# A quarter of the descriptor space for GpSimd's indirect transfers

## Chip, cores and metric

The kernel runs on one core of a Trainium2 chip. The metric is the device time of one execution in microseconds (us); of several runs the median counts. The engines are named as the profile names them: PE is TensorE (PEld its weight loads), DVE VectorE, ACT ScalarE, POOL GpSimd, SP SyncE; a q behind a name (POOLq, SPq) marks what the engine's sequencer does itself, such as semaphore instructions, DRAINs and the issue of DMAs.

## What is computed

Attention with a local window and a few global keys, and behind it a mixture of experts in which each token goes to one expert. Cut to what matters:

```python
# q, k, v: (4, 8, 768, 64); n_global 8, n_local 96; N = 3072 tokens, D = 512, E = 8 experts, F = 1024
scores = q @ k.T / 8 + alibi_bias            # kept where global, or 0 <= row - col < 96
a = softmax(where(keep, scores, -1e9))
x = (a @ v) as (N, D)
logits = x @ w_gate + modality_bias[modality_id]
e_idx = argmax(logits); gate_w = softmax(logits)[e_idx]
for e in range(E):
    mask = e_idx == e
    out[mask] = gate_w[mask] * (relu(x[mask] @ w1[e]) @ w2[e])
```

## The kernel before

*Attention stage.* 24 steps of 128 query rows each (`step`, four batches of six). A step loads `qt`, `kt`, `va`, `vl` on SyncE's queue, makes scores `s` (line 209), a biased minimum on VectorE (224), the exponential on ScalarE (240), transposes `pr` (254), multiplies by the values (279, 290) and writes 128 rows to `x_rows` in device memory (328). Gate logits and the routing are worked in between: for each token a row of its own in the list `ids_sorted`, sorted by expert, is written by GpSimd (`route_c`, 445), one indirect transfer for 128 tokens, 24 in all.

*Expert stage.* Eleven slots of one expert's tokens each: three of 256 tokens that start before the attention ends (e0 to e2), three of 512 (b0 to b2), two of 256 (c0, c1) and three small ones (g0 to g2, the last of 32 rows), in the order e0, e1, e2, b0, g0, b1, g1, c0, b2, c1, g2. For each slot SyncE loads the sorted token numbers (632) and the weights (660, 662), GpSimd gathers the tokens' rows from `x_rows` 128 at a time (`gather_x`, 640, 25 transfers), TensorE transposes them (`x_t`, 699), ScalarE and VectorE split rows and weights in a high and a low part (`split`, 686 and 687), TensorE multiplies (717 to 719 or 733 to 735, then 776 to 778), and `fin` scales the result on ScalarE (845) and writes its rows to `out` with an indirect transfer of GpSimd (846, 25 transfers). So GpSimd makes 74 indirect transfers: 24, 25 and 25, all but two of them of 128 rows.

*Order.* TensorE's and ScalarE's order is written out by hand (`manual_schedule`), in the attention stage VectorE's and GpSimd's too. SyncE's order, and in the expert stage VectorE's and GpSimd's, is set by a planner when the kernel is built.

*Storage.* The descriptor space of GpSimd's indirect transfers lies at the bottom of each partition, 16,384 bytes by default (line 1592 passes no size). Above it come the constants and small pools, then the attention pools `a1` (57,088 bytes: `kt`, `va`, `vl`, `tbl`, `pr`), `pp` (29,952 bytes: `qt`, `sc`, `pT`, `xr`, `xT`) and `a2` (9,024 bytes). The pools of the expert stage are laid from the other end downwards: `mp`, `wraw`, `wspa`, `xgp` and `idp` down to byte 117,152, and once the attention pools are closed `wspb` (76,192 to 117,152; the third cast of an expert's second weight matrix goes to 92,576 to 96,672), `wrawb` and `mp2` (down to 35,232). Where they lie over closed attention pools, the first user of a tile waits for the last user of the tiles below it (`reuse_waits="tile"`).

*Closing.* Behind the last slot each engine reads a flag and branches over a part that runs only for other inputs (1566, 1567); then come the closing waits, DRAINs and barriers of all engines, which the profile puts down to line 1637.

## Time and profile before

| | us |
|---|---|
| median of 3 runs (lowest, highest) | 444.78 (444.1, 445.35) |
| the profiled execution's own time | 443.69 |
| its span, from the first to the last instruction | 441.8 |
| TensorE busy | 426.5 |
| VectorE busy | 287.7 |
| ScalarE busy | 256.8 |
| GpSimd busy | 104.4 |

All rows are of the profiled execution. Busy time counts arithmetic and GpSimd's transfers, not the sequencers' work. A stretch of the span in which an engine is busy all the time is limited by that engine; one in which no engine is busy is limited by waits, which stand with the sequencers.

### The profile page before, as it was taken

What the parts mean: (1) busy time and instruction counts of PE and PEld (TensorE: products, weight loads), DVE (VectorE), ACT (ScalarE), POOL (GpSimd) and SP (SyncE); (2) the same over time, 40 slices, a digit from 0 to 9 for tenths busy, and PEclk for the clock granted to TensorE, in tenths of its full rate; (3) what the DMA queues carried; (4) which work ended last, traced back from release to release, by engine and by line L of the source; (5) the groups of instructions that cost most, each with busy time, mean ns of one, the idle gap of its engine ahead of it and who ended that gap; (6) DMA issues with size and microseconds to landing.
All of it is one profiled execution on the core that took longest, in us unless ns stands there. A gap on an engine that the chain in (4) does not pass through costs nothing.

```text
span 441.8 us, 12144 instructions
## 1 busy us (share of the span) xinstructions
PE 426.5 (97%) x4584; PEld 363.5 (82%) x4584; DVE 287.7 (65%) x1000; ACT 256.8 (58%) x511; POOL 104.4 (24%) x173
## 2 busy tenths in 40 slices
PE   8899999999999999999999999999999999999990
PEld 7788898898888989898888788887889888879850
DVE  7787887789798589999895347355355735702500
ACT  5888888888885374546446357345374644513420
POOL 6010023122523367241211133000332220011010
PEclk9999999999999999999999999999999999999997
DMA  8999999998878467659129767536667662351510
GB/s 241 314 317 349 359 333 322 319 287 263 275 242 304 168 218 299 208 164 357 55 61 343 286 197 222 199 97 203 216 202 256 219 216 96 118 214 49 192 35 27
DMA packets 53155, 97.63 MB, mean 221 GB/s; under 512 B 8143, under 2 KB 21967, under 8 KB 53088
## 3 DMA queue, kind: packets, MB, share of 16 engines
q1 hardware_dynamic: 48416, 83.92, 57.5%
q0 software_dynamic: 4672, 12.85, 8.0%
q8 instruction: 38, 0.62, 0.6%
q14 instruction: 29, 0.24, 0.2%
HBM read 82.37 MB, written 14.45 MB: 219 GB/s over the span
## 4 chain that ended last, share of the span: by engine, by line
PE 71%; issue 18%; POOL 3%; ACT 2%; DVE 2%; DMA 1%; POOLq 0%; SPq 0%
PE pt L254 7%; PE s L209 7%; PE x L290 6%; PE phb L718 3%; PE phb L719 3%; PE phb L717 3%; PE x L279 3%; PE pob L776 3%; PE tx L335 3%; PE phe L733 3%; PE pob L777 3%; PE pob L778 3%; PE phe L735 3%; PE phe L734 3%; PE poe L776 3%
## 5 line engine op out<-in xcount | busy, mean ns | idle before, releaser
L240 ACT ACTIVATE pr<-sc,nmx 128x168 f32<-128x168 f32 x192 | 67.6, 427 | 9.4 <-DVE nmx L224 6.8
L224 DVE CUSTOM_DVE_ANT_0 sc<-s,tbl 128x168 f32<-128x168 f32 x192 | 53.0, 329 | 16.7 <-PE s L209 15.0
L209 PE MATMUL s<-kt,qt 64*64 64x168 f32 x768 | 39.7, 313 | 0.6 <-DVE nmx L224 0.6
L254 PE MATMUL pt<-ident,pr 128*128 128x128 f32 x288 | 36.9, 277 | 1.1 <-issue 1.1
L719 PE MATMUL phb<-xhb,alb 128*128 128x512 f32 x96 | 37.8, 393 | 0.0
L718 PE MATMUL phb<-xlb,ahb 128*128 128x512 f32 x96 | 37.6, 392 | 0.0
L717 PE MATMUL phb<-xhb,ahb 128*128 128x512 f32 x96 | 37.6, 391 | 0.0
L846 POOL DMA_INDIRECT out<-obb,oib x12 | 12.6, 1047 | 99.5 <-ACT obb L845 97.7
L254 PEld LDWEIGHTS pt<-ident,pr 128*128 128x128 f32 x288 | 31.0, 141 | 5.9 <-issue 5.0
L209 PEld LDWEIGHTS s<-kt,qt 64*64 64x64 f32 x768 | 30.2, 133 | 6.4 <-DVE nmx L224 2.2
L261 ACT COPY pT<-pt 128x512 f32<-128x512 f32 x52 | 29.6, 588 | 8.0 <-PE pt L254 7.2
L445 POOL DMA_INDIRECT ids_sorted<-tki,pi x24 | 24.8, 1033 | 39.4 <-ACT pr L240 28.0
L290 PE MATMUL x<-va,pT 128*64 128x65 f32 x768 | 27.7, 224 | 0.0
L733 PE MATMUL phe<-xhe,ahe 128*128 128x256 f32 x96 | 27.5, 287 | 0.0
L734 PE MATMUL phe<-xle,ahe 128*128 128x256 f32 x96 | 27.2, 283 | 0.0
L735 PE MATMUL phe<-xhe,ale 128*128 128x256 f32 x96 | 27.2, 283 | 0.0
L290 PEld LDWEIGHTS x<-va,pT 128*64 128x64 f32 x768 | 24.4, 137 | 1.6
L721 ACT ACTIVATE hhb<-phb 128x256 fp32r<-128x256 f32 x24 | 9.3, 386 | 26.4 <-PE phb L719 26.4
L722 DVE SCALAR_TENSOR_TENSOR hlb<-phb,hhb 128x256 fp32r<-128x256 f32 x24 | 10.1, 422 | 20.6 <-ACT hhb L721 20.5
L718 PEld LDWEIGHTS phb<-xlb,ahb 128*128 128x128 f32 x96 | 18.0, 188 | 4.5 <-DVE xlb L703 0.4
L719 PEld LDWEIGHTS phb<-xhb,alb 128*128 128x128 f32 x96 | 18.0, 188 | 3.9
L717 PEld LDWEIGHTS phb<-xhb,ahb 128*128 128x128 f32 x96 | 18.0, 188 | 3.9
(408 smaller groups left out, 1146.0 us busy)
## 6 DMA issues: line engine op xcount, KB each, us to landing
va<-in_vr SPq DMA_DIRECT2D x24, 520.0 KB
kt<-in_ks SPq DMA_DIRECT2D x24, 272.0 KB
qt<-in_qs SPq DMA_DIRECT2D x24, 256.0 KB
x_rows<-xr SPq DMA_DIRECT2D x24, 256.0 KB
vl<-in_vo SPq DMA_DIRECT2D x48, 81.2 KB
rawe0a<-in_moe_w SPq DMA_DIRECT2D x4, 512.0 KB
rawe0b<-in_moe_w SPq DMA_DIRECT2D x4, 512.0 KB
rawe1a<-in_moe_w SPq DMA_DIRECT2D x4, 512.0 KB
```

Of the source, the lines that this page charges most:

```text
L209: nc.tensor.matmul(ps[g][64 * half : 64 * half + 64, c0 : c0 + W], qt[hs, hp, 64 * half : 64 * half + 64], kt[hs, hp, w0 : w0 + W], start= ...
L224: V.tensor_tensor_reduce(out=sc, in0=pss[n][g][:, c0 : c0 + W], in1=(tbl0 if n % NB == 0 else tbl)[:, hh, :], op0=ALU.add, op1=ALU.min, sc ...
L240: last[0] = nc.scalar.activation(pr[:, h * (PRW - W) : h * (PRW - W) + W], scs.pop((n, hh)), AF.Exp, bias=blk[n][:, hh : hh + 1], scale=-1.0,)
L254: nc.tensor.transpose(tp[:, j * P : (j + 1) * P], prs[(NP * n + hp) % NPR][:, o : o + P], ident)
L261: last[0] = nc.scalar.copy(pT.rearrange("p a b -> p (a b)"), tp)
L290: nc.tensor.matmul(px[h][64 * half : 64 * half + 64, hp * D1 : (hp + 1) * D1], pT_of(n, hp, 2 * h)[:, 64 * half : 64 * half + 64], va[r][: ...
L717: nc.tensor.matmul(ph, hi[:, fs], s.xh[:, c, :], start=(c == 0), stop=False)
L718: nc.tensor.matmul(ph, hi[:, fs], s.xl[:, c, :], start=False, stop=False)
L719: nc.tensor.matmul(ph, lo[:, fs], s.xh[:, c, :], start=False, stop=(c == 3))
L733: nc.tensor.matmul(o, hi[:, fs], s.xh[:, c, :], start=(c == 0), stop=False)
L734: nc.tensor.matmul(o, hi[:, fs], s.xl[:, c, :], start=False, stop=False)
L735: nc.tensor.matmul(o, lo[:, fs], s.xh[:, c, :], start=False, stop=(c == 3))
```

## The change

The program is built with a descriptor space of 4,096 bytes of each partition for GpSimd's indirect transfers, in place of the default of 16,384. Nothing else is edited. The constants and the attention pools, which are laid from below, come to lie 12,288 bytes lower (of `xr`, for instance, 104,832 to 110,976 becomes 92,544 to 98,688); the pools of the expert stage keep their places.

```diff
-    nc = _bacc.Bacc("TRN2", target_bir_lowering=False, num_devices=1)
+    nc = _bacc.Bacc("TRN2", target_bir_lowering=False, num_devices=1, dynamic_dma_scratch_size=4096)
```

## Rows read from the trace of the kernel before

**Rows 1.** The page: span, then busy us (share of the span) xinstructions

```profile
span 441.8 us, 12144 instructions
PE 426.5 (97%) x4584; PEld 363.5 (82%) x4584; DVE 287.7 (65%) x1000; ACT 256.8 (58%) x511; POOL 104.4 (24%) x173
```

**Rows 2.** Stretches: from:to, length, busy PE, PEld, DVE, ACT, POOL, clock, DMA, GB/s

```profile
136.00:142.00 6.00, 5.64 (x115) 4.67 (x110) 5.44 (x14) 3.75 (x7) 0.46 (x1) 1.00 0.73 240
142.00:240.00 98.00, 98.00 (x606) 86.14 (x607) 83.03 (x255) 50.09 (x76) 34.33 (x29) 1.00 0.59 208
240.00:418.00 178.00, 177.64 (x917) 148.14 (x919) 89.20 (x113) 87.17 (x128) 31.25 (x28) 1.00 0.56 187
431.00:441.80 10.80, 0.00 (x0) 0.00 (x0) 0.00 (x0) 0.69 (x1) 0.99 (x1) 0.73 0.08 28
```

**Rows 3.** GpSimd in order of time: start us, us, what, idle before it

```profile
193.96 0.98 POOL L640 DMA_INDIRECT xgb<-x_rows,uib  x1 [0.56 <-issue]
195.25 1.20 POOL L640 DMA_INDIRECT xgb<-x_rows,uib  x1 [0.30 <-issue]
...
431.98 0.99 POOL L846 DMA_INDIRECT out<-obc,oic  x1 [2.81 <-ACT obc L845]
```

**Rows 4.** Line 1567: operation xcount, ns min/median/max, first and last start us

```profile
L1567 POOLq INC_SWDGE_SEM  x1: 1675/1675/1675, 433.1 to 433.1; - x1
```

**Rows 5.** Line 1637, the closing instructions, columns as in rows 4

```profile
L1637 POOLq EVENT_SEMAPHORE  x4: 17/17/17, 441.0 to 441.7; - x4
L1637 POOLq DRAIN  x3: 46/107/6117, 434.8 to 441.5; - x3
L1637 SPq DRAIN  x3: 7/7/13, 435.7 to 441.2; - x3
...
L1637 PEldq DRAIN  x2: 8/8/8, 431.5 to 441.3; - x2
L1637 ACTq DRAIN  x2: 8/8/8, 434.3 to 441.2; - x2
```

**Rows 6.** SyncE's waits from 430 us on: us in total, times, longest

```profile
SPq L1637 <- PEq L1637: 5.9, 2, 5.4
SPq L1637 <- DMA out<-obc,oic: 0.2, 1, 0.2
```

**Rows 7.** Line 1592, the opening instructions, columns as in rows 4

```profile
L1592 POOLq DRAIN  x1: 194/194/194, 0.4 to 0.4; - x1
```

**Rows 8.** The indirect transfers by line, columns as in rows 4, and their landings

```profile
L445 POOL DMA_INDIRECT ids_sorted<-tki,pi x24: 956/973/1469, 69.6 to 175.4; - x24
...
L640 POOL DMA_INDIRECT xgb<-x_rows,uib x12: 949/1094/2022, 194.0 to 331.5; - x12
L640 POOL DMA_INDIRECT xge<-x_rows,uie x6: 954/1398/1841, 129.3 to 166.5; - x6
...
L640 POOL DMA_INDIRECT xgg<-x_rows,uig x3: 985/985/1504, 230.0 to 353.2; - x3
...
DMA to landing us min/median/max: 3.2/6.9/8.6
...
L846 POOL DMA_INDIRECT out<-obb,oib x12: 985/1006/1293, 249.7 to 403.9; - x12
L846 POOL DMA_INDIRECT out<-obe,oie x6: 985/1094/1433, 176.7 to 218.5; - x6
L846 POOL DMA_INDIRECT out<-obc,oic x4: 983/998/1036, 357.3 to 432.0; - x4
L846 POOL DMA_INDIRECT out<-obg,oig x3: 899/1022/1129, 275.9 to 428.3; - x3
```

**Rows 9.** Transposes of b0's rows, first block's casts, last write of rows, by start

```profile
206.16 0.60 PE L699 MATMUL mtb<-ident,xgb 128*128 128x128 f32 x4
...
154.04 1.99 ACT L686 CAST bhe<-rawe0b 128x1024 fp32r<-128x1024 f32 x2
...
143.29 0.35 SPq L328 DMA_DIRECT2D x_rows<-xr  x1
```

## Prediction

> **What bounds the kernel now.** I read the busy line of the page first: TensorE works for 426.5 of 441.8 us [rows 1]. The table by stretch then says where the other 15.3 us lie. Between 142 and 240 us TensorE lacks nothing, between 240 and 418 us 0.36 us, in the change of stages from 136 to 142 us 0.36 us; but from 431.0 to 441.8 us it does nothing at all [rows 2]. So no cost or saving on another engine moves the time in the body unless it makes TensorE wait, and there is one stretch of 10.8 us, the tail, in which the time is set by something else. That is where to look for a change that touches no matmul.
>
> In the tail the last scale and the last write of rows to `out` are over soon: GpSimd takes the last indirect transfer at 431.98 us for 0.99 us [rows 3], then an instruction of line 1567 for 1.675 us, to 434.8 us [rows 4]. The closing instructions, all put down to line 1637, show who is late: ScalarE's first DRAIN stands at 434.3, TensorE's at 431.5, SyncE's, which comes behind all its waits for transfers, at 435.7. GpSimd's first DRAIN starts at 434.8 and takes 6.117 us, to 440.9, and GpSimd's next semaphore instruction is at 441.0 [rows 5]. SyncE's last wait for a transfer is 0.2 us long, and then it stands 5.4 us for an engine [rows 6], which by these times is GpSimd (the view names another). So the rows have landed by 435.7 us and for the 5.3 us up to 441.0 the whole chip waits for one instruction of GpSimd.
>
> **What is in that instruction.** GpSimd has three more DRAINs, before its first transfer (0.194 us) and behind the long one (0.107 and 0.046 us) [rows 5, 7]. All four run with the same descriptor space, so its size alone isn't what takes 6 us; what differs is that 74 indirect transfers have gone since the DRAIN before: 24 scatters of token numbers, 25 gathers of rows, 25 writes of results [rows 8]. Nor is it the flight of the last one, by SyncE's 435.7. I take it that GpSimd goes through the records of the transfers that it still holds in that space, which costs 6.117/74 = 0.083 us each. In the body nothing says that it had to free records: the 74 take between 0.90 and 2.02 us [rows 8], at the end as at the start.
>
> **The change, part by part.** (1) *Fewer records at the end.* With a quarter of the space, GpSimd must free old records on the way, and holds fewer when it drains. How many isn't in the trace. Upper end of the gain: the DRAIN shrinks until SyncE's 435.7 us is late instead, 5.3 us. Lower end: the small space, too, holds all 74, no gain. If the default was just filled, a quarter of 74, 18.5, stays: 18.5 x 0.083 = 1.53 us, the DRAIN ends at 434.8 + 1.5 = 436.3 instead of 440.9, which is 4.6 us. I take 4.6, near the upper end, because a space that holds more than 74 at once is offset if old records are freed many at a time when it runs full; both ends stay for the range.
>
> The Trainium skill has sizes for this, which no row here shows. "DMA: Bandwidth & Descriptors", section "Terms", gives 16 bytes for a descriptor, and its section "The descriptor swizzle" nine per DMA engine for a transfer of 128 partitions. An estimate from that page: 4,096/16 = 256 places hold 28 such transfers, 16,384 bytes 113. If they were freed one at a time, 28 would be left, 2.3 us, and the gain 3.8 us; if all at once, at the 29th and the 57th, 18 would be left, and it is 4.6.
>
> (2) *The freeing moves into the body.* Some 55 records x 0.083 = 4.6 us of GpSimd's time, spread over transfers from 150 us on. GpSimd is busy for 24% of the span [rows 1]. The work that hides it is the matmuls between a gather and the transposes that read it. The tightest such gather behind the first 18 transfers is the first of block b0: issued at 193.96 us, transposed at 206.16; the longest landing of its kind is 8.6 us, so 206.16 - 193.96 - 8.6 = 3.6 us of cover [rows 3, 8, 9]. Even half of the 4.6 us in one place would stay under it. Cost 0; without that cover 1.0 us at most (4.6 - 3.6).
>
> (3) *A wait for space.* A transfer that finds the space full waits until an older one has landed. Lower bound 0: landings take at most 8.6 us and two starts on GpSimd are at least 1.2 us apart [rows 3, 8], so at most some 7 transfers are under way at once, against the 18 that a quarter holds at the least. Upper bound: it waits for all before it, 8.6 us. I take 0, since 7 is far from 18. Queued behind the waiting instruction on GpSimd are the next gathers, writes and scatters, and TensorE's transposes wait for the gathers alone.
>
> (4) *Storage.* The attention pools lie above the descriptor space and move down by 12,288 bytes; the expert stage's pools, laid from the other end, stay. So the expert tiles `bhe`, `ble`, the raw weights and `xhb` reuse storage of other attention tiles than before. The waits that this takes away can give TensorE at most its 0.36 us from 136 to 142 us [rows 2]. A new one: the third cast of the first block (the second of the pair at 154.04, so 155.1 us) now takes the place of the row tiles `xr`, whose last write starts at 143.29; with the longest landing of any row, 8.6 us, it is over at 151.9, 3.2 us earlier [rows 9]. I take 0, between -0.4 and +0.4. Instructions are neither added nor removed in the source; the planner may order SyncE, VectorE and GpSimd anew in the expert stage, which the same 0.36 us bound as gains and which I leave in the range as a loss of up to 0.5 us.
>
> Sum: -4.6 + 0 + 0 + 0. On the profiled execution's 443.69 us (span 441.8 and 1.9 around it) that is 439.1. The median of the runs is 444.78, 1.1 us higher, so the forecast there is 440.2 us.
>
> **The rivals.** *The DRAIN doesn't shrink:* its 6.1 us are a fixed price once any transfer has gone, or all 74 still fit. For it: there is no row with a DRAIN behind a few transfers. Against it: nothing has been left to wait for since 435.7, and a fixed price of that size shows in none of the other three. Time: 444.8, no change. The Trainium skill speaks for this: "VectorE: DVE Perf Modes", section "The DRAIN you can't avoid", counts the DRAINs at a program's start and end as boilerplate of about 12 ns on every engine, whatever the kernel. By that rule the descriptor space couldn't matter and the time would be 444.8; the trace agrees for ScalarE (8 ns) and SyncE (7 to 13 ns) and differs for GpSimd's 6,117 ns [rows 5].
>
> *Only part goes:* records are freed one by one and 25 to 57 of the 74 stay: 6.117 - 25 x 0.083 = 4.0 us down to 6.117 - 57 x 0.083 = 1.4 us of gain, 440.8 to 443.4, some 442 us. The trace has nothing for or against.
>
> *The small space stalls GpSimd:* a full space makes it wait for everything in it to land, just ahead of b0's first gather, and the DRAIN stays. 8.6 us less the 3.6 us of cover is 5.0 us in which TensorE stands: 449.8 us. It decides from a wait of 3.6 us on. Against it stand the 7 under way at most.
>
> **How the numbers follow.** Forecast (gain 4.0 to 5.3): 0.58. Part goes: 0.20. No change: 0.16. Stall: 0.06. About 0.3%, 1.3 us, is what a measurement of this kernel can tell from none; so faster 0.78, same 0.16, slower 0.06. Low end: the lowest run, 444.1, less 5.3 is 438.8. High end: with 3.8 it would be 441.0; to leave out no more than 2 in 10 it takes in the whole second rival, up to the border of no change, 443.4.
>
> **What the changed profile would show.** Step 1: GpSimd's long DRAIN on the closing line falls from 6.1 to about 1.5 us, and the stretch behind TensorE's last matmul from 10.8 to about 6.2; SyncE's first DRAIN stays some 4.7 us behind that matmul. Step 2: indirect transfers behind the first 18 take a little longer in sum, or a few take some us more. Step 3: TensorE's idle time from 142 to 418 us stays near 0.4 us. Step 4: casts and loads keep their order around 136 to 160 us. A DRAIN of 6 us again would make the forecast wrong in step 1; TensorE idle ahead of `mtb` would in step 3.

## The result and the profile after

The changed kernel takes 438.14 us in the median of 4 runs (437.77 to 440.06), the kernel before 444.44 us in 4 runs beside it (443.81 to 445.35). The ratio is 0.987, with a 95% interval of 0.984 to 0.990: faster, by 6.3 us between the medians. That is the way that was forecast and more of it, and 0.7 us below the low end of the range. The profiled execution took 440.06 us, of which the span is 438.0; that of the kernel before took 443.69 and 441.8.

First the busy line of the page after, against [rows 1]:

```profile
span 438.0 us, 12145 instructions
PE 426.7 (97%) x4584; PEld 363.9 (83%) x4584; DVE 287.3 (66%) x1000; ACT 256.8 (59%) x511; POOL 103.3 (24%) x173
```

No work has gone: TensorE's busy time differs by 0.2 us, GpSimd's by 1.1. The arithmetic, the loads and the transfers are the same on all five engines, and so is their order, but for two matmuls on TensorE that run side by side. So the 3.8 us by which the span is shorter are waits. The table by stretch shows whether they lay in the body (columns as in [rows 2]):

```profile
136.00:142.00 6.00, 4.35 (x78) 3.62 (x74) 4.76 (x12) 3.71 (x7) 0.62 (x1) 1.00 0.53 163
142.00:240.00 98.00, 98.00 (x644) 86.17 (x645) 83.15 (x254) 49.13 (x75) 34.34 (x29) 1.00 0.59 206
240.00:418.00 178.00, 177.57 (x902) 148.65 (x901) 89.33 (x114) 88.15 (x130) 30.18 (x28) 1.00 0.56 190
```

They didn't. From 142 to 418 us TensorE lacks 0.43 us, as before (0.36); in the change of stages it lacks 1.65 in place of 0.36, so the body of this profile is longer. TensorE's waits from 130 to 142 us name the 1.3 us:

```profile
PE lp L344 <- issue: 1.3, 1, 1.3
```

"issue" is time in which the engine waited for nothing that the profile shows. This row is in neither of the next two profiles of a kernel with 4 KB (e1, e2), so I don't put it down to the change.

What has gone lies in the tail. GpSimd's last transfer after, against [rows 3]:

```profile
433.50 0.99 POOL L846 DMA_INDIRECT out<-obc,oic  x1 [2.81 <-ACT obc L845]
```

And the closing instructions, against [rows 4] (line 1567) and [rows 5] (line 1637):

```profile
L1567 POOLq INC_SWDGE_SEM  x1: 395/395/395, 434.6 to 434.6; - x1
...
L1637 POOLq EVENT_SEMAPHORE  x4: 17/17/17, 437.2 to 437.9; - x4
L1637 POOLq DRAIN  x3: 46/107/1946, 435.1 to 437.8; - x3
L1637 SPq DRAIN  x3: 7/7/13, 437.2 to 437.5; - x3
...
L1637 PEldq DRAIN  x2: 8/8/8, 433.0 to 437.5; - x2
L1637 ACTq DRAIN  x2: 8/8/8, 435.9 to 437.5; - x2
```

Read them from the start of the last transfer. GpSimd's instruction of line 1567 falls from 1.675 to 0.395 us, its long DRAIN from 6.117 to 1.946. The DRAIN now ends 435.1 + 1.9 = 437.0, and SyncE, whose DRAIN stands behind its waits for transfers, is there at 437.2: SyncE is the last one now. From the last transfer's start to GpSimd's next semaphore instruction it was 441.0 - 432.0 = 9.0 us and is 437.2 - 433.5 = 3.7, so 5.3 us less. From TensorE's DRAIN to the end of the span it was 441.8 - 431.5 = 10.3 us and is 438.0 - 433.0 = 5.0, again 5.3 less. The profiles' difference, 3.8, is this 5.3 less the 1.5 us by which this body is longer.

SyncE's waits from 430 us on show the same turn, against [rows 6]:

```profile
SPq L1637 <- DMA out<-obc,oic: 1.5, 1, 1.5
SPq L1637 <- PEq L1637: 0.7, 2, 0.5
```

It waits 1.5 us for the landing of the last rows. Its two waits for the other engines come to 0.7 us in place of 5.9: one of 0.5 us stands in both profiles, and the one of 5.4 us is down to 0.2.

### The profile page after: what moved, and what is told of

Its sections match the earlier page's. It is cut to its first block, busy times and chain, and to the rows that moved or that the text cites. A ratio compares the mean times of both kernels' runs of the same rounds, so it can differ in the third digit from the quotient of the medians.

```text
span 438.0 us, 12145 instructions
## 1 busy us (share of the span) xinstructions
PE 426.7 (97%) x4584; PEld 363.9 (83%) x4584; DVE 287.3 (66%) x1000; ACT 256.8 (59%) x511; POOL 103.3 (24%) x173
## 4 chain that ended last, share of the span: by engine, by line
PE 73%; issue 18%; ACT 2%; POOL 2%; DVE 2%; DMA 1%; POOLq 0%; SPq 0%; DVEq 0%
PE s L209 8%; PE pt L254 7%; PE x L290 6%; PE phb L718 3%; PE phb L719 3%; PE phb L717 3%; PE x L279 3%; PE pob L776 3%; PE tx L335 3%; PE phe L733 3%; PE pob L777 3%; PE pob L778 3%; PE phe L735 3%; PE phe L734 3%; PE poe L776 3%
## 5 line engine op out<-in xcount | busy, mean ns | idle before, releaser
L279 PE MATMUL x<-vl,pT 40*64 40x65 f32 x768 | 20.5, 222 | 1.5 <-ACT pT L261 0.8
```

The source lines that it names most:

```text
L279: nc.tensor.matmul(px[h][64 * half : 64 * half + 64, hp * D1 : (hp + 1) * D1], pT_of(n, hp, 1)[hs, 64 * half : 64 * half + 64], vl[r][hs, ...
```

## The experiments

The theory: GpSimd keeps a record of each indirect transfer until it frees it, pays at the end by the number of records that it still holds, and a small space makes it free them on the way. The rivals: it pays by the size of the space, not by the count; the other storage gives a part; the body is faster too. For the first, two profiles decide nothing: a DRAIN of 0.56 us and 0.35 for each KB goes through both.

**e1, the changed kernel again.**

> The changed kernel once more, 4 KB of descriptor space. Theory: the end alone is shorter, by 5.3 us (from the last indirect transfer's start to GpSimd's next semaphore instruction 9.0 us before, 3.7 us after); the rest of the 6.3 us between the first medians is spread from run to run. Then the difference of the medians comes down towards 5.3 us with more runs, a time of about 438.7 against 444.2, and the 1.3 us that TensorE stood at 136 us in the first profile is not there, or is elsewhere. Rival: the body is faster too, by 1 us; then the difference stays at 6.3 us.

Measured: 443.82 us (6 runs) against 449.33 (11 runs) of the kernel before on that chip, so 5.5 us; ratio 0.9866 (0.9839 to 0.9893). The line-1567 instruction took 0.396 us, the DRAIN 1.962; from TensorE's last matmul to the end 5.59 us, where the kernel before has 10.83. All profiles of one kernel have the same end within some 0.2 us (10.83 twice before; 5.57, 5.59 and 5.79 after); what moves between them is the body.

**e2, 4 KB with every tile in its old place.**

```diff
-    warm = const.tile([P, P], BF16, name="warm")
+    warm = const.tile([P, P + 6144], BF16, name="warm")[:, 0:P]
```

> 4 KB of descriptor space, and 12,288 unused bytes above it, so that every tile lies where it lies in the kernel before. Theory: the storage does nothing; the same time as the changed kernel in the same call within 0.7 us, and the same closing DRAIN of about 1.9 us and line-1567 instruction of 0.4 us. Rival, the moved pools give about 1 us of the gain: the time is 1 us above the changed kernel's, with the same end.

Measured: 443.41 us, ratio 0.9865 (0.9827 to 0.9903) beside e1's 0.9866; 0.396 and 1.987 us at the end. The 12,288 bytes by which the pools move have no part in the gain that these runs can tell.

**e3 and e4, 8 KB and 2 KB.**

```diff
-    nc = _bacc.Bacc("TRN2", target_bir_lowering=False, num_devices=1, dynamic_dma_scratch_size=4096)
+    nc = _bacc.Bacc("TRN2", target_bir_lowering=False, num_devices=1, dynamic_dma_scratch_size=8192)
```

> 8 KB of descriptor space. Theory, GpSimd pays by the record still held: with 8 KB it frees once, at about the 57th transfer, and some 25 are left: a DRAIN of 2.1 us at 0.083 each (2.9 if there is a fixed part of 1.3 us), a line-1567 instruction of 0.6 us, and one indirect transfer that starts about 1 us late. Rival, it pays by the size of the space: the two profiles at 16 and 4 KB give 0.56 us and 0.35 us for each KB, so 3.3 us for the DRAIN, and 0.8 us for the other. Time by the first 438 to 439, by the second 440.

> 2 KB of descriptor space. Theory, by the record: about 11 left, as with 4 KB, so the DRAIN stays at 1.9 us and the line-1567 instruction at 0.4; more freeing on the way, each time shorter (some 0.2 us before a transfer); the time is that of the changed kernel, since SyncE's waits set the end. Rival, by the size: a DRAIN of 1.25 us and 0.2 us. Second rival, a space that small makes a transfer wait for earlier ones to land: single indirect transfers start microseconds late and TensorE stands, over 440.

Line 1567 and the closing DRAINs of e3, then of e4 (columns as in [rows 4]):

```profile
L1567 POOLq INC_SWDGE_SEM  x1: 696/696/696, 438.6 to 438.6; - x1
...
L1637 POOLq DRAIN  x3: 46/107/2477, 439.3 to 442.4; - x3
L1637 SPq DRAIN  x3: 7/7/13, 441.3 to 442.1; - x3
```

```profile
L1567 POOLq INC_SWDGE_SEM  x1: 416/416/416, 438.6 to 438.6; - x1
...
L1637 POOLq DRAIN  x3: 46/107/2017, 439.0 to 441.7; - x3
L1637 SPq DRAIN  x3: 7/7/13, 441.1 to 441.4; - x3
```

With 2 KB the two instructions are those of 4 KB (e1), and even 0.02 and 0.06 us longer, where a price by size wanted 1.25 us: that rival falls. With 8 KB the DRAIN is 2.48, not 3.3, but 0.4 more than 25 x 0.083; and the transfer that was to start 1 us late isn't there. Ratios 0.9870 (0.9837 to 0.9903) and 0.9857 (0.9828 to 0.9886): the times can't tell the three sizes apart, the ends can (from the last matmul 6.21 us with 8 KB, 5.63 with 2 KB).

**e5, 16 KB and a DRAIN in the middle.** This one keeps the space and takes the records away.

```diff
                     tc.declare_no_dep(ins.ins, prev.ins, reason="each token has a row of its own")
                 fins.append(ins)
+            if s.name == "c0" and t == 1:
+                behind(nc.gpsimd.drain(), ins)
```

> 16 KB of descriptor space as before, and one DRAIN of GpSimd added in the expert stage, right behind the 67th indirect transfer, ahead of some 30 us in which GpSimd has nothing to do. Theory, GpSimd pays by the record still held: the added DRAIN takes 5.6 us (0.62 + 67 x 0.0743, from the profiles at 16 and 8 KB) where nobody waits; at the end 7 records are left: the line-1567 instruction takes 0.34 us (0.195 + 7 x 0.02), the closing DRAIN about 1.9 us and ends some 0.47 us behind the last landing; the time is that of the 4 KB kernel, 0.988 of the kernel before. Rival, it pays by the size of the space: the end stays at 1.7 and 6.1 us and the time too.

The added DRAIN (line 859) and the end (1569 is 1567 of the kernel before, 1639 is 1637):

```profile
L859 POOLq DRAIN  x1: 5533/5533/5533, 365.0 to 365.0; - x1
...
L1569 POOLq INC_SWDGE_SEM  x1: 342/342/342, 436.3 to 436.3; - x1
...
L1639 POOLq DRAIN  x3: 46/107/1837, 436.6 to 439.4; - x3
L1639 SPq DRAIN  x3: 7/7/13, 438.8 to 439.1; - x3
```

The price has moved to 365.0 us, behind 67 transfers, at 5.533/67 = 0.083 us each, and the table by stretch shows that TensorE doesn't feel it:

```profile
365.00:371.00 6.00, 6.00 (x28) 4.90 (x27) 2.84 (x5) 2.48 (x5) 0.00 (x0) 1.00 0.11 26
```

The time is 442.32 us against 446.96, ratio 0.9899 (0.9870 to 0.9928), and the end 5.55 us from the last matmul, as with 4 KB. So neither the small space nor the storage is needed for the gain: it is enough that few records are left.

**e6 and e7, 16 KB with 22 transfers more and 22 fewer.**

```diff
+    spare = nc.dram_tensor("spare", (NT, DM), F32, kind="Internal").ap()
...
                 fins.append(ins)
+            if s.straight and s.name not in ("c1", "g2"):
+                nc.gpsimd.indirect_dma_start(
+                    out=spare,
+                    out_offset=bass.IndirectOffsetOnAxis(ap=s.oi[0:r, t : t + 1], axis=0),
+                    in_=ob[0:r],
+                    in_offset=None,
+                    bounds_check=NT - 1,
+                    oob_is_err=False,
+                )
```

> 16 KB as before, and 22 indirect transfers more: each 128-row write of results is made a second time, to a tensor that nobody reads (but for the last slot's two, and the 32-row one), so 96 in all. Theory, by the record: a line-1567 instruction of 2.1 us (0.195 + 96 x 0.02), a closing DRAIN of 7.75 us (0.62 + 96 x 0.0743), and the time 2.1 us longer than the kernel before. Rival, by the size of the space: 1.7 and 6.1 us again, and no longer time.

```diff
             nc.scalar.mul(ob[0:r], s.po[t][0:r], gate)
+            if s.straight and s.name not in ("c1", "g2"):
+                continue
             ins = nc.gpsimd.indirect_dma_start(
```

> 16 KB as before, without those 22 writes of results, so that most rows of the output are never written; 52 indirect transfers. Theory, by the record: 1.24 us and 4.5 us, and the time 2.1 us shorter than the kernel before. Rival, by the size of the space: 1.7 and 6.1 us again, and the same time.

The end of e6 (1577 and 1647 are its lines), then of e7:

```profile
L1577 POOLq EVENT_SEMAPHORE  x3: 17/17/43, 439.1 to 439.3; - x3
L1577 POOLq COMPARE_BRANCH  x1: 50/50/50, 436.5 to 436.5; - x1
L1577 POOLq INC_SWDGE_SEM  x1: 2092/2092/2092, 439.4 to 439.4; - x1
...
L1647 POOLq DRAIN  x3: 46/107/7914, 441.6 to 450.0; - x3
```

```profile
L1569 POOLq INC_SWDGE_SEM  x1: 1228/1228/1228, 436.6 to 436.6; - x1
...
L1639 POOLq DRAIN  x3: 46/107/4321, 437.8 to 442.7; - x3
```

Both instructions follow the count at one size of the space: 2.09 and 7.91 us with 96 transfers, 1.23 and 4.32 with 52, expected 2.1 and 7.75, 1.24 and 4.5. e7's time does too: 2.3 us shorter (ratio 0.9944, 0.9922 to 0.9967), expected 2.1. e6's time doesn't: 7.5 us longer (1.0188, 1.0148 to 1.0229), expected 2.1. The end, from TensorE's last matmul on, is 15.47 us in its profile, 4.6 more than before. Of this 2.2 us are the two instructions, and 2.4 a later start of the first of them, most of it a pause of GpSimd on line 1577: 2.6 us from the branch at 436.5 to the next instruction at 439.1, which is 0.5 us in the kernel before (432.3 to 432.8). The other 2.9 us lie ahead of the end, where 22 more transfers, and another order of the planner's, can each have a part; this and the pause stay open.

**e8, the kernel before again.**

> The kernel before once more, for a second profile of it: the end as in the first (an instruction of 1.68 us on line 1567, a DRAIN of 6.1 us, 10.8 us from TensorE's last matmul to the end). Theory, what differs between profiles of one kernel is the first 160 us: TensorE's last matmul moves by some us from profile to profile for either kernel. Rival, the body is shorter with 4 KB: the last matmul is later in all profiles of the kernel before than in all of the changed one on the same chip.

The same end: 1.676 and 6.117 us, and 10.83 from the last matmul. TensorE's last matmul ends at 433.4 us here, at 430.9 in the first profile: for one kernel, in two profiles, 2.4 us lie in the body. On e8's chip it ends at 434.1 in e5, whose end is as short as with 4 KB, and in the first pair of profiles at 432.5 with 4 KB; both are later than in the kernel before, so no profile shows a shorter body and the rival has nothing for it.

**e9, 4 KB and three transfers fewer.** The two freeings that the profiles at 4 KB show, ahead of the 50th and 72nd transfer (below), say that many records go at once. Then the count left depends on where the last freeing falls, and fewer transfers can leave more.

```diff
             nc.scalar.mul(ob[0:r], s.po[t][0:r], gate)
+            if s.straight and (s.name, t) in (("e0", 0), ("e0", 1), ("e1", 0)):
+                continue
             ins = nc.gpsimd.indirect_dma_start(
```

> 4 KB of descriptor space, and three of the first writes of results left out (both of e0, the first of e1), so that 384 rows of the output are never written; 71 indirect transfers. Theory: GpSimd frees many records at once, when the space is full (in the profiles at 4 KB ahead of the 50th and the 72nd transfer), so that the number left at the end is a saw-tooth: with 71 the last freeing doesn't come and some 29 are left, against 10 with 74. Then the line-1567 instruction takes 0.195 + 29 x 0.02 = 0.78 us; the closing DRAIN ends 0.05 + 29 x 0.041 = 1.24 us behind the last landing, or behind 29 x 0.041 us from its own start if that is later: 4.4 us behind the start of the last transfer, where 74 transfers give 3.5. So three transfers fewer make the end 0.6 us longer. Rival, records are freed one by one, or the count left at the end is always some 10: 0.4 us, 3.5 us, and the end as with 74.

```profile
L1569 POOLq INC_SWDGE_SEM  x1: 775/775/775, 439.4 to 439.4; - x1
...
L1639 POOLq DRAIN  x3: 46/107/2555, 440.2 to 443.3; - x3
L1639 SPq DRAIN  x3: 7/7/13, 442.2 to 443.0; - x3
```

0.775 us where 0.78 was expected, and the DRAIN ends 4.50 us behind the start of the last transfer, expected 4.4; GpSimd is behind SyncE again, by 0.6 us. The saw-tooth stands, and the freeing one by one falls.

**e10, the changed kernel a third time.**

> The changed kernel a third time, for the difference of the times alone. Theory: nothing but the end is shorter, by 5.2 us, 0.988 of the kernel before; the 6.3 us between the first medians is spread. Rival: the body is about 1 us faster too, 0.986; then the difference over all runs of the changed kernel stays above 6 us.

Measured: 444.56 us against 448.73, 4.2 us, ratio 0.9892 (0.9866 to 0.9919). The kernels whose end SyncE sets have by now six differences of medians from the kernel before: 6.3 (the first), 5.5, 5.9 (e2), 5.9 (e4), 4.6 (e5) and 4.2; their mean is 5.4, with a standard error of 0.3 (or a little more, since three of them share the runs of the kernel before). The end alone gives 5.2. So the 6.3 of the first comparison holds about 1 us of spread, and a faster body isn't needed.

**The price of the end.** For each profile, in us from the start of the last transfer; the last landing is the last semaphore event of that transfer in the trace. "Held" is the count since the last DRAIN where nothing is freed (16 KB); the line-1567 instruction lies for those on 0.204 + 0.0197 x held (fitted to e5 and e6; it gives 1.66 for 74 and 1.23 for 52), and for the others "held" is worked out from it.

| | space | transfers | line-1567 instruction | held | DRAIN from | last landing | DRAIN to |
|---|---|---|---|---|---|---|---|
| before | 16 KB | 74 | 1.675 | 74 | 2.83 | 3.07 | 8.95 |
| e6 | 16 KB | 96 | 2.092 | 96 | 5.68 | 3.25 | 13.60 |
| e7 | 16 KB | 52 | 1.228 | 52 | 2.39 | 3.07 | 6.71 |
| e5 | 16 KB | 7 since a DRAIN | 0.342 | 7 | 1.51 | 3.01 | 3.35 |
| e3 | 8 KB | 74 | 0.696 | 25 | 1.85 | 3.25 | 4.33 |
| e9 | 4 KB | 71 | 0.775 | 29 | 1.95 | 3.26 | 4.50 |
| after | 4 KB | 74 | 0.395 | 10 | 1.55 | 3.03 | 3.50 |
| e4 | 2 KB | 74 | 0.416 | 11 | 1.57 | 3.09 | 3.59 |

One rule gives all eight ends within 0.01 us: the DRAIN takes 0.041 us for each record held, waits for the last landing if that is later, and then takes 0.041 for each once more, and 0.05. For 74: 2.83 + 3.03 + 3.03 + 0.05 = 8.94. For 10: 3.03 + 0.41 + 0.05 = 3.49. With 8 KB: 3.25 + 1.03 + 0.05 = 4.33, so e3's missing 0.4 us was the landing, which cuts into the first pass. The rule was read out of the profiles up to e8; e9 was forecast with it and agrees. The four profiles that repeat a kernel's end (e1, e2, e8, e10) follow it too; in e10 the last rows land at 3.25 us where they landed at 3.03 in the first profile of that kernel, and the DRAIN ends at 3.71 for 3.50. All but two of the transfers are of 128 rows, so these runs can't tell a price by the transfer from one by its rows. That GpSimd really goes through its records twice is what the numbers look like; no view shows the inside of that instruction.

## Why the prediction was right and wrong

*What bounds the kernel.* Right: the tail alone has moved, and SyncE's waits for the last landing are next, as the upper end of step 1 said (5.3 us; 5.3 in the first profile, 5.2 over all).

*Step 1, fewer records.* The mechanism is right, and e5 to e7 show it: the price goes by the records held. Three sizes in it were off. First, the count left: I took 18.5 and 10 are left. The space is freed down to some 7 records when it is full (22 transfers lie between the freeings at the 50th and the 72nd, and 10 left at the end are the 72nd to 74th and 7), and a quarter of 74 had no row behind it. The Trainium skill's sizes, in "DMA: Bandwidth & Descriptors", sections "Terms" and "The descriptor swizzle", gave 28 transfers for 4 KB by an estimate; e9's 29 held agree with that but for one (two of the 71 are of 32 rows), though the page counts for a transfer of 1 MiB and a gather of 128 rows here is 256 KB. Second, the price of the DRAIN: 0.083 each is right only where the first pass outlasts the landing. With 10 it took 1.95 us, not 0.83, since it can't end before the landing and 0.46 us more. Third, I read the instruction of line 1567 [rows 4] and left its 1.675 us as it was. It too goes by the records, at 0.02 us each, and 1.28 us of it went.

What each is worth, by the rule behind the table, in us from the start of the last transfer, where SyncE is done at 3.65: with 10 records and the old 1.675 us the DRAIN ends at 2.83 + 0.41 + 0.41 + 0.05 = 3.70, so the right count alone gives nearly the whole 5.3. With my 18.5 records and a line-1567 instruction that shrinks with them, to 0.57, it ends at 3.03 + 0.76 + 0.05 = 3.84: 5.1. With both as I had them it ends at 2.83 + 0.76 + 0.76 + 0.05 = 4.40: 4.6, my forecast. So two terms of this step were mis-sized, the count left (18.5 for 10) and the line-1567 instruction (no change for 1.28 us), and either alone would have brought the gain to SyncE's bound within 0.2 us.

*The rule of the Trainium skill against it,* in "VectorE: DVE Perf Modes", section "The DRAIN you can't avoid": by its about 12 ns for the DRAINs at a program's start and end nothing could have changed. ScalarE's (8 ns) and SyncE's (7 to 13 ns) agree with it after as before; GpSimd's went from 6.117 to 1.946 us. The page speaks of DRAINs of the runtime, and the profile puts these down to a line of the kernel; whether they are the ones it means isn't shown.

*Step 2, the freeing in the body.* Right that it costs nothing, and sized some four times too high: I spread 4.6 us, and the two freeings that show cost 1.0 us together. What GpSimd shows is two late starts, here the first, 4.85 us behind the transfer before it where the kernel before waits 4.37 us, both ended by the same transposes:

```profile
272.10 0.98 POOL L640 DMA_INDIRECT xgg<-x_rows,uig  x1 [4.85 <-PE mtb L699]
```

```profile
270.09 0.98 POOL L640 DMA_INDIRECT xgg<-x_rows,uig  x1 [4.37 <-PE mtb L699]
```

The second, ahead of the 72nd, is 18.82 for 18.32 us. So 0.5 us for some 22 records. e1 and e2 have both within 0.02 us, e3 has neither. The 0.02 us that this makes for each record is no fixed price: in e4 the same transfer starts 0.3 us late,

```profile
275.86 0.98 POOL L640 DMA_INDIRECT xgg<-x_rows,uig  x1 [4.68 <-PE mtb L699]
```

and with 2 KB a freeing is of fewer records: some 7, by an estimate from the others (half of the 29 that 4 KB held, less the 7 that stay); counted back by sevens from the 11 left, one falls on this transfer. That points to a fixed part in each freeing; no run shows it by itself. A first freeing with 4 KB, due at about the 29th transfer, and that of 8 KB, due at about the 57th, leave no mark; both would fall on a transfer that follows another at once. Why they leave none isn't settled. TensorE's 0.43 us from 142 to 418 us show the cover.

*Step 3, no wait for space.* Right, down to 2 KB: e4's profile shows no late start but the 0.3 us above.

*Step 4, the storage.* Right: e2 undoes it and has the same ratio.

*The rivals.* That the DRAIN doesn't shrink (6.117 to 1.946 us), that records are freed one by one so that 25 or more stay (10 did, and e9's count rose with fewer transfers) and that the space stalls GpSimd (e4) are all out.

*The numbers.* On the profiled 443.69 us the forecast was 439.1, and 5.3 in place of 4.6 makes 438.4. I then added 1.1 us, because the median lay so far above the profiled run, and took the low end as the lowest run less 5.3. Both treat four executions as firmer than they are: runs of the changed kernel lie from 437.77 to 440.06, and differences of medians of one and the same gain came out between 4.2 and 6.3 us. The range lacked that spread of about 1 us on its low side; with the 5.2 us that the end gives, the forecast would have been 444.78 - 5.2 = 439.6, inside the range. So: direction and place right; the gain 4.6 for 5.2 because of the two terms of step 1; the rest of the miss is spread.

## What to carry to other kernels

Look at what GpSimd does behind its last indirect transfer: each transfer whose record it still holds cost 0.02 us in one closing instruction here and 0.041 in the DRAIN behind the last landing, or 0.083 where the DRAIN's first pass outlasts that landing, on the path that ends the kernel; freed on the way, some 22 cost 0.5 us together, under cover of TensorE's work. A smaller descriptor space or a DRAIN in a stretch where GpSimd is idle takes that off; below about 13 records (0.041 each and 0.05, against the 0.6 us that SyncE takes behind the landing) nothing more is to be had, and the count left is a saw-tooth in the number of transfers, so it has to be worked out, or read from the line-1567 instruction, for each kernel. And an instruction of unknown price in the tail, next to the one that a change attacks, may go by the same count: treat it as a term of the sum, with both ends.

## What the runs showed of the hardware that was not expected

GpSimd's closing DRAIN has no fixed price, and the descriptor space none of its own: 0.34 us behind the last landing with 7 records, 10.4 with 96. By the rule that fits its ends, its two parts, before and after the landing, cost the same 0.041 us a record. The freeings that show are of many records at once: with 4 KB some 22, in about 0.5 us. And TensorE stood 1.3 us at 136 us in one profile of the changed kernel, and GpSimd 2.6 us behind a branch in e6, with nothing in the profile that they waited for.
